# A two-dimensional Fourier filter gated by a feed-forward block: the narrow hidden tile's down products packed into row groups, the variances' roots as a power on GpSimd, and the head's steps in another order

## The chip, the cores and the metric

The kernel runs on one core of a Trainium2 chip. The metric is the device time of one execution in microseconds (us); the time before is the median of three runs. A second source is one profiled execution, in which every instruction of every engine has a start, a duration and the event that released it. The engines are PE (TensorE: matmuls, with PEld for its weight loads), DVE (VectorE), ACT (ScalarE), POOL (GpSimd) and SP (SyncE, which issues most of the DMAs). Each engine works through its own queue in the order in which it was written.

## The reference

The input `x` has 2048 rows of 512 values, all float32. Each row is normalised; the normalised rows go through two branches whose product is added to `x`.

```python
xn = (x - mean(x)) / sqrt(var(x) + 1e-5)            # per row
s  = irfft2(rfft2(xn) * (w_r + 1j * w_i))           # 2048 x 512 spectral filter
gate, up = xn @ W_gate, xn @ W_up                   # 512 -> 1376
g  = silu((gate * (gate > 0) * up) @ W_down)        # 1376 -> 512
out = x + s * g
```

## The kernel before

**Number format.** Every float32 operand of a large matmul is split into a float16 high part and a float16 low part, and a product is made of three passes: high x high, high x low and low x high (`PASSES`, line 24). A matmul here is one 128-column weight load and a stream of up to 512 columns.

**Feed-forward branch.** The 2048 rows form four blocks of 512 (`NBL`), each of four row tiles of 128. The 1376 hidden columns form eleven tiles: ten of 128 and a last one of 96 (`TAIL`, `fwidth`, line 58). For a block `c` and a tile `f`, `product` (line 683) makes gate and up in PSUM, twelve matmuls of 512 columns each; `rectify` (line 735) takes the positive part of the gate on ACT; `hidden` (line 741) multiplies on DVE and splits the result into a high part (ACT) and a low part (DVE), in the tile `h16`. `down` (line 758) then accumulates, for each row tile `i`, three matmuls of 512 columns per hidden tile into one PSUM tile `dn`; for the narrow tile these contract 96 of the 128 rows. After the eleventh tile `gate` (line 774) applies SiLU on ACT. `ff_steps` (line 782) lists these steps for blocks 1 to 3; block 0 is written out at lines 1079 to 1096.

**Spectral branch.** `fold` and `split` (lines 435 and 464) prepare pairs of row tiles on DVE and ACT, `first_stage` (line 472) makes the first transform, `fft_chunk` (line 805) eight chunks of the middle ones through DRAM, `last_stage` and `finish` (lines 965 and 1022) the inverse and the output.

**Head.** For the first two pairs of row tiles (`c` = 0 and 1) `stats` (line 318) takes mean and variance on DVE. `deviation` (line 329) forms 16 / sqrt(var + eps): a square root on ACT, and on DVE a reciprocal, one refining step and the product of mean and scale with its sign turned. `normalise` (line 370) then makes `xf`, here on ACT (`NORM`, line 37). `turn_row` (line 416) transposes each row on PE into the tile `head` and splits it into `xT`, high on ACT, low on DVE. The gate and up weights come in seven groups (tiles `raw`); `squares`, `group_scale` and `group_split` (lines 507 to 565) find a power of two for each tile and split it (tiles `m`, `sum`, `p`, `wgu`). For pairs 2 to 7 `deviations` (line 352) does four rows' roots at once on DVE, by an integer estimate and three refining steps. While PE has nothing to do in the head, `keep_busy` (line 406) gives it matmuls whose result (`idle`) nobody reads.

**Down weights.** `load_down` (line 586) loads W_down, `down_scale` (line 593) finds its scale and `down_weights` (line 615) splits each hidden tile's weights into the two halves of `wds`, high on ACT and low on DVE.

**Order.** All of this is entered as steps in a planner (`Plan`, line 77). A step has an engine, an assumed cost, names that it reads and writes, and a due time, set by hand (the constants of lines 33 to 47) or from the steps that need it. The planner goes through time, lets each engine begin the step that is due first among those that can begin, counts the buffers of each kind (`k4`: 12, `F`: 2, `gu`: 2, `dn`: 2 and so on; `F`, `gu` and `dn` lie in PSUM, an `F` tile takes two banks, the others one) and so writes one fixed order per engine. `ORDER` (line 42, empty) can replace single due times. A step with `port=True` is not planned at the same time on DVE and POOL.

Of the kernel before, what the change touches and what calls it, by code (L numbers as in the profile page):

```python
# [7 lines left out]
F16 = mybir.dt.float16  # L8
# [235 lines left out]
def kernel(ctx: ExitStack, tc: tile.TileContext, x, w_in, wd, wd_tail, wl, ew, sp, c_r, c_d, c_m, c_x, c_s, out):  # L244
# [42 lines left out]
    T = Plan({"k4": 12, "k2": 10, "h16": NFT, "xg": NBL + 1, "F": 2, "gu": 2, "dn": 2, "q": 4, "q4": 2, "mv": 4, "m": 4, "p": 4, "am": 1, "mid": 3})  # L287
# [41 lines left out]
    def deviation(c):  # L329

        tile_of(f"q{c}", "q", [P, 4, 2], F32)

        def first():
            q = T[f"q{c}"]
            DVE.tensor_scalar(q[:, 0], T[f"mv{c}"][:, :, 1], EPS, -4.0 / XS ** 2, op0=ALU.add, op1=ALU.mult)

        def last():
            ve, sq, y, t = (T[f"q{c}"][:, i, :] for i in range(4))
            DVE.reciprocal(y, sq)
            for i in range(2):  # L340
                DVE.scalar_tensor_tensor(t[:, i:i + 1], y[:, i:i + 1], ve[:, i:i + 1], y[:, i:i + 1],
                                         op0=ALU.mult, op1=ALU.mult)
            DVE.scalar_tensor_tensor(y, t, 3.0, y, op0=ALU.add, op1=ALU.mult)
            if "ACT" in NORM[c]:
                DVE.scalar_tensor_tensor(ve, T[f"mv{c}"][:, :, 0], -1.0, y, op0=ALU.mult, op1=ALU.mult)
        step("DVE", .13, first, reads=[(f"mv{c}", 0), (f"mv{c}", 1)], writes=[(f"q{c}", 0)], port=True)
        step("ACT", .11, lambda: ACT.activation(T[f"q{c}"][:, 1], T[f"mv{c}"][:, :, 1], AF.Sqrt, bias=eps, scale=4.0 / XS ** 2),
             reads=[(f"mv{c}", 0), (f"mv{c}", 1)], writes=[(f"q{c}", 1)])
        step("DVE", .78 + .14 * ("ACT" in NORM[c]), last, reads=[(f"q{c}", 0), (f"q{c}", 1)], writes=[(f"q{c}", 2)], port=True)
        return f"q{c}", 0  # L350

    def deviations(cs):


        name = f"q{cs[0]}"
        tile_of(name, "q4", [P, 3, 4], F32)

        def run():
            w, y, t = (T[name][:, i, :] for i in range(3))
            b = T[name].bitcast(I32)  # L360
            for j, c in enumerate(cs):
                DVE.tensor_scalar(w[:, 2 * j:2 * j + 2], T[f"mv{c}"][:, :, 1], EPS, 64.0 / XS ** 2, op0=ALU.add, op1=ALU.mult)
            DVE.tensor_scalar(b[:, 1, :], b[:, 0, :], -0.5, float(0x5F3759DF), op0=ALU.mult, op1=ALU.add)
            for n in range(3):
                DVE.scalar_tensor_tensor(t, y, -(4.0 ** -n), y, op0=ALU.mult, op1=ALU.mult)
                DVE.tensor_mul(t, t, w)
                DVE.scalar_tensor_tensor(y, t, 3.0, y, op0=ALU.add, op1=ALU.mult)
        step("DVE", 2.4, run, reads=[(f"mv{c}", i) for c in cs for i in range(2)], writes=[(name, 2)], port=True)
# [413 lines left out]
    def ff_steps(c, lag=6):  # L782
# [8 lines left out]
        for f, i in [(f, i) for i in range(2) for f in range(NFT - lag, e - i)] + [(e, 0), (e - 1, 1), (e, 1)]:  # L791
            down(c, f, (i,))
            if f == e:
                gate(c, i)
# [4 lines left out]
        for f, i, part in order:  # L799
            down(c, f, (i,), part)  # L800
            if f == e:
                gate(c, i, part)
# [430 lines left out]
```

## Time and profile before

| | us |
|---|---|
| median of three runs (409.93 to 410.04) | 410.02 |
| profiled execution, its own time | 409.73 |
| profiled execution, span from first to last instruction | 407.9 |
| PE busy (3056 matmuls) | 402.5 |
| DVE busy | 303.9 |
| ACT busy | 191.0 |
| POOL busy | 54.1 |

The profiled execution's own time is 1.8 us above its span, and 0.3 us below the median. PE's busy time contains 10.9 us of the `idle` matmuls, all in the first 20 us. The records of matmuls overlap (a matmul of 512 columns is shown with 379 ns, and the next starts about 216 ns later), so PE's speed is read from the distance between starts. All instructions carry the same source line, that of the helper which keeps them in order, so they are told apart by their tiles: `dn<-wds,h` is a down product, `xf<-x,q` a normalisation, `gu<-xT,wgu` a gate or up product.

### The profile page before, as it was taken

Reading aid. Unit: us, or ns where it says so; the run is one execution under the profiler, and the core shown is the slowest. Engines: PE = TensorE matmul, PEld = TensorE weight load, DVE = VectorE, ACT = ScalarE, POOL = GpSimd, SP = SyncE. Lnnn points to the kernel's source line nnn. Section 1 sums busy time; section 2 is a strip of 40 time slices with the busy share of each in tenths; the row PEclk is TensorE's granted clock in tenths of the full one; section 3 lists DMA queues with packets and bytes.
Section 4 is the critical chain, followed back from the end, with each engine's and each line's share of the span. In section 5 each row is a group of like instructions: output and inputs, shape, how many; then the busy total and the mean of one; then the engine's idle time right before and its main releaser. Section 6 shows DMA issues by size and latency. Waiting matters only on the chain.

```text
span 407.9 us, 7730 instructions
## 1 busy us (share of the span) xinstructions
PE 402.5 (99%) x3056; PEld 213.9 (52%) x3056; DVE 303.9 (74%) x648; ACT 191.0 (47%) x361; POOL 54.1 (13%) x68
## 2 busy tenths in 40 slices
PE   8999999999999999999999999999999999999996
PEld 7784444444444444446555456555554444444445
DVE  5897999999999972416985578965882329988953
ACT  5989944634435584123344434443424236442211
POOL 0000000000000000003430031500230009351400
PEclk9999999999999999999999999999999999999999
DMA  8963042007544799800005550066002598335321
GB/s 303 416 238 103 2 114 94 0 2 154 156 104 120 251 202 251 310 2 3 1 2 167 169 169 2 1 191 176 24 0 53 125 230 240 129 130 182 123 85 53
DMA packets 35237, 51.74 MB, mean 127 GB/s; under 512 B 15424, under 2 KB 17184, under 8 KB 35200
## 3 DMA queue, kind: packets, MB, share of 16 engines
q1 hardware_dynamic: 34912, 50.71, 41.6%
q8 instruction: 24, 0.39, 0.4%
q10 hardware_dynamic: 288, 0.52, 0.4%
q14 instruction: 13, 0.11, 0.1%
HBM read 35.48 MB, written 12.60 MB: 118 GB/s over the span
## 4 chain that ended last, share of the span: by engine, by line
PE 94%; ACT 2%; DVE 2%; DMA 1%; issue 0%
PE gu L70 54%; PE dn L70 27%; PE s L70 3%; PE z L70 3%; PE xx L70 3%; PE y L70 2%; PE v L70 2%; DMA x<-in_x 1%; ACT wgu L70 1%; ACT xf L70 1%; PE dn_3bb L70 0%; PE dn_3b L70 0%; DVE wgu L70 0%; DVE q L70 0%; ACT xT L70 0%; DVE st L70 0%
## 5 line engine op out<-in xcount | busy, mean ns | idle before, releaser
L70 PE MATMUL gu<-xT,wgu 128*128 128x512 f16 (+1 forms) x1032 | 214.3, 364 | 0.3 <-DVE xT L70 0.3
L70 PEld LDWEIGHTS <-wgu 128*128 128x128 f16 x1032 | 99.5, 98 | 104.3 <-issue 3.8
L70 PE MATMUL dn<-wds,h 128*128 128x512 f16 (+2 forms) x528 | 116.3, 373 | 0.0
L70 PEld LDWEIGHTS <-h 128*128 128x128 f16 (+1 forms) x594 | 54.0, 98 | 57.0 <-issue 2.6
L70 ACT ACTIVATE h<-h 128x512 f16<-128x512 f32 (+1 forms) x44 | 27.5, 628 | 66.7 <-DVE h L70 66.7
L70 POOL TENSOR_TENSOR po<-tt,tt 128x256 f32<-128x256 f32 x16 | 15.4, 964 | 273.7 <-DVE tt L70 273.7
L70 DVE TENSOR_TENSOR h<-gu,r 128x512 f32<-128x512 f32 (+2 forms) x52 | 33.6, 647 | 23.1 <-PE gu L70 20.8
L70 ACT ACTIVATE r<-gu 128x512 f32<-128x512 f32 (+1 forms) x44 | 26.1, 594 | 30.6 <-PE gu L70 30.0
L70 DVE TENSOR_TENSOR h<-h,h 128x512 f16<-128x512 f32 (+1 forms) x44 | 29.8, 689 | 7.8 <-ACT h L70 7.8
L70 POOL TENSOR_TENSOR ae<-zz 128x128 f32<-128x128 f32 (+1 forms) x32 | 26.3, 855 | 54.5 <-ACT zz L70 54.5
L70 DVE SCALAR_TENSOR_TENSOR tt<-xsp,cw,wt 128x512 f32<-128x512 f32 x32 | 25.9, 856 | 0.0
L70 ACT ACTIVATE g<-dn,cdi 128x512 f32<-128x512 f32 (+1 forms) x16 | 10.6, 673 | 26.7 <-PE dn L70 26.6
L70 DVE TENSOR_TENSOR a<-y,a 128x1024 f16<-128x1024 f32 x8 | 9.8, 1220 | 16.1 <-ACT a L70 15.9
L70 DVE TENSOR_TENSOR t<-v,t 128x1024 f16<-128x1024 f32 x8 | 9.8, 1220 | 13.2 <-ACT t L70 13.2
L70 DVE TENSOR_TENSOR sv<-sv,g 128x512 f32<-128x512 f32 (+2 forms) x18 | 11.8, 680 | 8.8 <-ACT g L70 8.8
L70 PE MATMUL gu<-xT,wgt 128*64 128x256 f16 (+1 forms) x144 | 17.0, 309 | 0.0
L70 DVE SCALAR_TENSOR_TENSOR wgu<-raw,p,wgu 128x512 f16<-128x512 f32 x20 | 14.4, 746 | 0.2 <-ACT wgu L70 0.2
L70 ACT ACTIVATE zz<-s,cwi 128x1024 f32<-128x1024 f32 x8 | 8.7, 1112 | 11.8 <-PE s L70 9.2
L70 ACT ACTIVATE wgu<-raw 128x512 f16<-128x512 f32 x20 | 12.3, 619 | 2.9 <-DMA raw<-in_w 2.9
L70 PEld LDWEIGHTS <-wgt 128*64 128x64 f16 (+1 forms) x144 | 9.6, 106 | 7.3 <-issue 1.9
L70 DVE BATCH_NORM_STATS2 st<-x 128x6 f32<-128x512 f32 x16 | 10.8, 674 | 3.4 <-DMA x<-in_x 3.4
L70 DVE TENSOR_TENSOR z<-z,z 128x1024 f16<-128x1024 f32 x8 | 9.8, 1219 | 4.7 <-ACT z L70 4.7
(138 smaller groups left out, 433.0 us busy)
## 6 DMA issues: line engine op xcount, KB each, us to landing
A_d<-t SPq DMA_DIRECT2D x16, 256.0 KB, 3.4
rw<-in_wl SPq DMA_DIRECT2D x8, 512.0 KB, 3.7
wt<-in_wl SPq DMA_DIRECT2D x8, 512.0 KB, 5.0
at<-A_d SPq DMA_DIRECT2D x8, 512.0 KB, 5.1
C_d<-t SPq DMA_DIRECT2D x16, 256.0 KB, 3.3
ct<-C_d SPq DMA_DIRECT2D x16, 256.0 KB, 7.6
xt<-in_x SPq DMA_DIRECT2D x16, 256.0 KB, 2.9
out<-xt SPq DMA_DIRECT2D x15, 256.0 KB, 2.1
```

The lines of the kernel that those rows point to most:

```text
L70: return lambda *args, **kw: self.tc.keep_in_program_order(f(*args, **kw))
```

## The change

Three things change together. The first is the narrow tile in blocks 0 to 2 (`WHOLE = 3`). Its three passes contract 3 x 96 = 288 rows, which are now laid out as 128 + 128 + 32. The first two parts are matmuls over all 128 rows; their weights stand in `wds[:, TAIL, 0]` and `wds[:, NFT, 0]`, and `hidden` places copies of the high part and the low part beside each other in `h16`. The last 32 rows (low part of hidden columns 64 to 95) of the four row tiles are stacked in a new tile `hc`, and `down_rest` multiplies them in four matmuls, one in each group of 32 rows of the array, into four PSUM banks. For that, rows 2 and 3 of blocks 0 to 2 share an `F` tile (before, block 0 only), and all four gates of a block come after `down_rest`. W_down's last 96 rows are passed in three arrangements, the tail's DMAs are now two (256 KB, and 512 KB into a `k4` tile), and `down_weights` gets two more steps on ACT and two on DVE.

The second is the root. `deviation` and `deviations` become additions of eps, a power of -0.5 and a multiplication by 16 on POOL; the first square root's table on ACT is no longer asked for, and the table of SiLU is asked for at the start.

The third is the order: pair 0 is normalised on DVE, 86 due times, most of them of the head, are replaced by `ORDER`, and several due times set by hand are different, among them those of the first stage (from 18.18 + 17.03 k to 52.05 + 13.03 k), of the folds (`FOLD_LEAD` from 92.09 to 33.39) and of the last stage (from 275.37 + 10.87 k to 311.66 + 6.53 k).

```diff
-T0, DOWN, FIRST, FIRST_STEP, MID, MID_STEP, LAST, LAST_STEP = 0.15, 43.88, 18.18, 17.03, 171.03, 5.03, 275.37, 10.87
+T0, DOWN, FIRST, FIRST_STEP, MID, MID_STEP, LAST, LAST_STEP = 0.15, 44.8, 52.05, 13.03, 170.04, 4.98, 311.66, 6.53
-FOLDS, FOLD_LEAD, MARGIN = ['DVE', 'DVE', 'DVE', 'DVE', 'DVE', 'DVE', 'DVE', 'DVE'], 92.09, 1.89
+FOLDS, FOLD_LEAD, MARGIN = ['DVE', 'DVE', 'DVE', 'DVE', 'DVE', 'DVE', 'DVE', 'DVE'], 33.39, 1.9
-NORM, TURN1 = (('ACT', 'ACT'), ('ACT', 'ACT')), 'PE'
+NORM, TURN1 = (('DVE', 'DVE'), ('ACT', 'ACT')), 'PE'
-ORDER = {}
+ORDER = {"ACT ('x0', 1)": 8.03, "DVE ('mv0', 0)": 22.85, ... "DVE ('xf0', 0)": -2.56, "DVE ('xf0', 1)": -1.23, ... "DVE ('xf0', 2)": 61.96, ...}
+SMALL = .6, .3
+WHOLE = 3
...
-    eps = cpool.tile([P, 1], F32, name="eps")
-    DVE.memset(eps, 4.0 * EPS / XS ** 2)
-    ACT.activation(warm, ones[:, 0:1], AF.Sqrt)
+    half = cpool.tile([P, 4], F32, name="half")
+    DVE.memset(half, -0.5)
+    ACT.activation(warm, ones[:, 0:1], AF.Silu)
...
-        step("DVE", .13, first, ...)
-        step("ACT", .11, lambda: ACT.activation(T[f"q{c}"][:, 1], T[f"mv{c}"][:, :, 1], AF.Sqrt, bias=eps, scale=4.0 / XS ** 2),
-        step("DVE", .78 + .14 * ("ACT" in NORM[c]), last, ...)
+        def root():
+            POOL.tensor_scalar(r(), T[f"mv{c}"][:, :, 1], EPS, None, op0=ALU.add)
+            POOL.tensor_tensor(r(), r(), half[:, 0:2], op=ALU.pow)
+            POOL.tensor_scalar(y(), r(), XS, None, op0=ALU.mult)
+        step("POOL", SMALL[0] + SMALL[1], root, ...)
+        if "ACT" in NORM[c]:
+            step("DVE", .16, lambda: DVE.scalar_tensor_tensor(shift(), T[f"mv{c}"][:, :, 0], -1.0, y(), op0=ALU.mult, op1=ALU.mult),
...
             for j, c in enumerate(cs):
-                DVE.tensor_scalar(w[:, 2 * j:2 * j + 2], T[f"mv{c}"][:, :, 1], EPS, 64.0 / XS ** 2, op0=ALU.add, op1=ALU.mult)
-            DVE.tensor_scalar(b[:, 1, :], b[:, 0, :], -0.5, float(0x5F3759DF), op0=ALU.mult, op1=ALU.add)
-            for n in range(3):
-                DVE.scalar_tensor_tensor(t, y, -(4.0 ** -n), y, op0=ALU.mult, op1=ALU.mult)
-                DVE.tensor_mul(t, t, w)
-                DVE.scalar_tensor_tensor(y, t, 3.0, y, op0=ALU.add, op1=ALU.mult)
+                POOL.tensor_scalar(r[:, 2 * j:2 * j + 2], T[f"mv{c}"][:, :, 1], EPS, None, op0=ALU.add)
+            POOL.tensor_tensor(r, r, half, op=ALU.pow)
+            POOL.tensor_scalar(y, r, XS, None, op0=ALU.mult)
...
-        step("SP", .6, lambda: SP.dma_start(wdr[:fwidth(n), NFT, :], wd_tail), writes=[("wd", NFT)], lead=22, kb=192)
+        step("SP", .6, lambda: SP.dma_start(wdr[:, NFT, :], wd_tail[:, 0, :]), writes=[("wd", NFT)], lead=22, kb=256)
+        tile_of("wrest", "k4", [P, 2, D], F32)
+        step("SP", .6, lambda: SP.dma_start(T["wrest"], wd_tail[:, 1:3, :]), writes=["wrest"], lead=22, kb=512)
...
+        first, second = wds[:, TAIL, 0, :], wds[:, NFT, 0, :]
+        step("DVE", stt(512), lambda: less(first, wdr[:, NFT, :], slice(96, P)), ...)
+        step("ACT", act(512) + .1, lambda: ACT.activation(second, T["wrest"][:, 0, :], AF.Copy, scale=sc[:, TAIL:NFT]), ...)
+        step("DVE", stt(512), lambda: less(second, T["wrest"][:, 0, :], slice(0, 64)), ...)
+        step("ACT", act(512) + .1, lambda: ACT.activation(wds[:, NFT, 1, :], T["wrest"][:, 1, :], AF.Copy, scale=sc[:, TAIL:NFT]), ...)
...
+        if f == TAIL and c < WHOLE:
+            tile_of(f"hc{c}", "hc", [P, P], F16)
+            for k, (slot, to, of) in enumerate(((0, 96, 0), (1, 0, 32), (1, 32, 64))):
+                step("ACT", act(512), lambda slot=slot, to=to, of=of: ACT.activation(h16()[to:to + 32, slot], h32()[of:of + 32], AF.Copy), ...)
+            step("DVE", dve(512), lambda: DVE.tensor_sub(h16()[64:, 1], h32()[0:64], h16()[0:64, 0]), ...)
+            def low():
+                for i in range(4):
+                    DVE.tensor_sub(T[f"hc{c}"][32 * i:32 * i + 32], h32()[64:96, i], h16()[64:96, 0, i])
+            step("DVE", .8, low, ...)
+            return
...
+                if packed:
+                    for h in range(2):
+                        matmul(t, T[f"h16_{c}_{f}"][:, h, i, :], wds[:, TAIL + h, 0, cols], start=False, stop=False)
+                    continue
...
+    def down_rest(c):
+        names = [down_name(c, i) for i in range(4)]
+        def run():
+            for i, name in enumerate(names):
+                rows = slice(32 * i, 32 * i + 32)
+                matmul(T[name][:, i - 2, :] if i >= 2 else T[name], T[f"hc{c}"][rows, :], wds[rows, NFT, 1, :], start=False, stop=True)
+        step("PE", .25, run, mode=4, reads=[f"hc{c}", "wdr"], writes=list(dict.fromkeys(names)), due=tick(.25))
...
+        if c < WHOLE:
+            down_rest(c)
+            for i in range(4):
+                gate(c, i)
```

More of the change, by code (lines that the diff above doesn't have):

```diff
@@ L383, in normalise @@
             e = engines[i]
-            step(e, .62 if e == "ACT" else pool1(512) if e == "POOL" else dve2(512), lambda i=i: run(i), reads=[*x_names(c, i), (f"mv{c}", i), (q, 2)],
+            step(e, .72 if e == "ACT" else pool1(512) if e == "POOL" else dve2(512), lambda i=i: run(i), reads=[*x_names(c, i), (f"mv{c}", i), (q, 2), (q, 0)],
                  writes=[(f"xf{c}", i)], port=e != "ACT", due=HEAD[2 * c] if c < 2 else None)
@@ L617, in down_weights @@
             e = fwidth(f)
-            step("ACT", act(512) + .1, lambda f=f, e=e: ACT.activation(wds[:e, f, 0, :], wdr[:e, f + 1, :], AF.Copy, scale=sc[:e, f:f + 1]),
+            step("ACT", act(512) + .1, lambda f=f: ACT.activation(wds[:, f, 0, :], wdr[:, f + 1, :], AF.Copy, scale=sc[:, f:f + 1]),
                  reads=[("wd", f + 1), "scd"], writes=[("wd", f)])
@@ L622, in down_weights, with less @@
                 reads=[("wd", f + 1), ("wd", f), "scd"], writes=[("wdl", f)])
+        def less(to, of, rows):
+            DVE.scalar_tensor_tensor(to[rows], of[rows], sc[rows, TAIL:NFT], to[rows], op0=ALU.mult, op1=ALU.subtract)
+        first, second = wds[:, TAIL, 0, :], wds[:, NFT, 0, :]
+        step("DVE", stt(512), lambda: less(first, wdr[:, NFT, :], slice(96, P)), port=True, reads=[("wd", NFT), ("wdl", TAIL), "scd"], writes=[("wd", TAIL)])
+        step("ACT", act(512) + .1, lambda: ACT.activation(second, T["wrest"][:, 0, :], AF.Copy, scale=sc[:, TAIL:NFT]),
+             reads=["wrest", "scd"], writes=[("wd", NFT)])
+        step("DVE", stt(512), lambda: less(second, T["wrest"][:, 0, :], slice(0, 64)), port=True, reads=["wrest", ("wd", NFT), "scd"], writes=[("wdl", NFT)])
+        step("ACT", act(512) + .1, lambda: ACT.activation(wds[:, NFT, 1, :], T["wrest"][:, 1, :], AF.Copy, scale=sc[:, TAIL:NFT]),
+             reads=["wrest", ("wd", NFT), "scd"], writes=["wdr"])
     def filter_scale(due):
@@ L770, in run @@
                            start=f == 0 and n == 0, stop=f == NFT - 1 and n == 2)
-        cost = pe(3 * len(rows), cols.stop - cols.start)
-        step("PE", cost, run, reads=[("wd", f), ("wdl", f), (f"h16_{c}_{f}", 0), (f"h16_{c}_{f}", 1)], writes=names, due=tick(cost))
+        cost = pe((2 if packed else 3) * len(rows), cols.stop - cols.start)
+        w = [("wd", f), ("wdl", f)] + [("wd", NFT), ("wdl", NFT)] * packed
+        step("PE", cost, run, reads=[*w, *((f"h16_{c}_{f}", k) for k in range(5 if packed else 2))], writes=names, due=tick(cost))
+    def down_rest(c):
[5 more added lines that the diff above has]
+        step("PE", .25, run, mode=4, reads=[f"hc{c}", "wdr"], writes=list(dict.fromkeys(names)), due=tick(.25))
     def gate(c, i, part=0):
-        name, cols = "dn0_23" if c == 0 and i >= 2 else f"dn{c}_{i}" + "b" * part, columns(c, i)[part]
+        name, cols = down_name(c, i, part), columns(c, i)[part]
         if f"g{c}" not in T.tiles:
@@ L778, in gate @@
         step("ACT", act(cols.stop - cols.start) + .1, lambda: ACT.activation(
-            T[f"g{c}"][:, i, cols], T[name][:, i - 2, :] if name == "dn0_23" else T[name], AF.Silu, scale=cdi),
+            T[f"g{c}"][:, i, cols], T[name][:, i - 2, :] if name.endswith("_23") else T[name], AF.Silu, scale=cdi),
             reads=[name, "scd"], writes=[(f"g{c}", i, part)], due=clock[0] + 4)
@@ L792, in ff_steps @@
             down(c, f, (i,))
-            if f == e:
+            if f == e and c >= WHOLE:
                 gate(c, i)
@@ L1094 @@
             down(0, f, rows)
-        for i in rows:
-            gate(0, i)
+    down_rest(0)
+    for i in range(4):
+        gate(0, i)
     for c in range(1, NBL):
@@ L1218 @@
     wd = np.asarray(B_W_down)
[L1219 removed]
+    ins = [("x", xp), ("w", np.concatenate(wp, axis=1)), ("wd", wd[:n].reshape(TAIL, P, D).transpose(1, 0, 2)), ("wdt", np.stack([wd[n + r] for r in (np.r_[0:96, 0:32], np.r_[32:96, 0:64], np.tile(np.r_[64:96], 4))], axis=1)),
            ("wl", wl), ("ew", ew), ("sp", sp), ("c_r", c_r), ("c_d", c_d), ("c_m", c_m), ("c_x", c_x), ("c_s", c_s)]
```

43 lines of the change are left out of this document (19 added, 24 removed).

## The prediction

> **What bounds the kernel now.** I read the page first: the engines' busy time, share of the span and instructions.
>
> ```profile
> PE 402.5 (99%) x3056; PEld 213.9 (52%) x3056; DVE 303.9 (74%) x648; ACT 191.0 (47%) x361; POOL 54.1 (13%) x68
> ```
>
> PE sets the time: work that leaves PE's queue after the head shortens the run one for one, if PE doesn't begin to wait. Next come the stages, each with its length, then PE, PEld, DVE, ACT and POOL busy, the clock and the DMA share.
>
> ```profile
> 10.00:15.00 5.00, 4.71 (x45) 4.03 (x43) 4.41 (x13) 5.00 (x16) 0.00 (x0) 1.00 1.02 415
> 15.00:20.00 5.00, 4.50 (x40) 3.66 (x39) 4.32 (x14) 4.75 (x11) 0.00 (x0) 1.00 1.02 414
> 30.00:50.00 20.00, 20.00 (x101) 9.81 (x100) 17.51 (x40) 18.99 (x46) 0.00 (x0) 1.00 0.16 53
> 50.00:100.00 50.00, 50.00 (x331) 23.61 (x329) 48.16 (x119) 25.11 (x39) 0.00 (x0) 1.00 0.27 68
> 100.00:200.00 100.00, 100.00 (x725) 49.38 (x724) 70.30 (x183) 44.03 (x77) 4.31 (x5) 1.00 0.52 146
> ```
>
> From 20 us PE has no gap, at full clock. Before that ACT is the full engine (5.00 and 4.75 us of 5), DVE close to it, and the DMA engines are saturated. In 50 to 100 us DVE is 96% busy, so PE runs there without waiting only because the order suits it. The head, in the chain in order of time (start, length) and in the timeline:
>
> ```profile
> 6.16 0.30 ACT q L70
> 7.46 1.52 ACT xf L70 x2
> 8.98 1.84 ACT wgu L70 x5
> 10.82 0.97 ACT xT L70 x2
> 19.87 8.02 PE gu L70 x72
> ```
>
> ```profile
> 5.94 0.18 DVE L70 BATCH_NORM_AGGREGATE mv<-st 128x2 f32<-128x6 f32 x1
> 8.47 0.37 DVE L70 TENSOR_SCALAR p<-p 128x2 int32<-128x2 int32 x2
> 9.04 0.66 PE L70 MATMUL head<-cS,xf 128*128 128x128 f32 x4
> 10.12 0.71 ACT L70 ACTIVATE wgu<-raw,p 128x512 f16<-128x512 f32 x1
> 11.83 1.03 PE L70 MATMUL gu<-xT,wgu 128*128 128x256 f16 x8
> 13.15 1.47 PE L70 MATMUL gu<-xT,wgu 128*128 128x256 f16 x12 [0.29 <-DVE xT L70]
> 14.60 1.91 PE L70 MATMUL gu<-xT,wgu 128*128 128x256 f16 x16
> 17.12 1.47 PE L70 MATMUL gu<-xT,wgu 128*128 128x256 f16 x12
> ```
>
> Pair 0's variance is ready at 6.12 us, its scale at 7.46; ACT then holds the chain alone: normalise, squares and split of weights, copies of xT. Useful products begin at 11.83 and have no gap from 19.87. In those 8.04 us PE does 8 + 12 + 16 + 12 = 48 products of 256 columns; 72 of them take 8.02 us further on, so 48 are 5.35. Two groups of transposes take about 0.5 us each (from here: issued up to the next work, 0.1 below the 0.66 shown) and the scale sums 0.1. So about 1.5 us are lost after the start, and the start is late.
>
> **Part 1, the packed tile.** What PE pays, from chain rows of undisturbed and of mode-changing work:
>
> ```profile
> 117.05 1.29 PE dn L70 x6
> 312.16 2.59 PE gu L70 x12
> 212.44 2.70 PE gu L70 x12
> 221.66 0.77 PE v L70 x12
> ```
>
> A down product costs 1.29 / 6 = 0.215 us. A narrow tile costs a block 12 of them; now 8, and one round of four in four row groups. The trace has no such row groups, but `v` runs 64 x 64 tiles: 12 products of 512 columns in 0.77 us, that is three rounds of four at 0.215 (0.645) and 0.125 for entering the mode. Products behind a change of mode cost 2.70 instead of 2.59, so leaving costs 0.11. `down_rest` then costs 0.215 + 0.125 + 0.11 = 0.45 and a block saves 4 x 0.215 - 0.45 = 0.41 us; three blocks 1.23. Bounds: if the changes of mode fall beside others', 3 x 0.645 = 1.94 saved; if the four run one after another, 0.235 lost a block, 0.7 in all.
>
> The Trainium skill, "TensorE: Matmul & The Clock Gate", section "Measured speedup vs the span model", gives 3.07 instead of 4 for four row tiles of 32 at 512 columns. By that figure the round would be an estimated 0.28 us and three blocks would save about 1.0 us; the `v` row speaks for 4, and no run here shows 32-row groups yet.
>
> What the packing adds elsewhere, by groups (busy, mean ns):
>
> ```profile
> L70 ACT ACTIVATE h<-h 96x512 f16<-96x512 f32 x4 | 2.5, 630 | 12.9 <-DVE h L70 12.9
> L70 DVE TENSOR_TENSOR xs<-ee 128x128 f32<-128x128 f32 x16 | 3.6, 283 | 0.0
> L70 DVE SCALAR_TENSOR_TENSOR wds<-wds,scd 96x512 f16<-96x512 f32 x1 | 0.7, 742 | 0.0
> L70 ACT ACTIVATE g<-dn,cdi 128x512 f32<-128x512 f32 x15 | 10.1, 686 | 23.9 <-PE dn L70 23.9
> wds<-in_wdt SPq DMA_DIRECT2D x1, 192.0 KB, 12.1
> ```
>
> Each block: three more copies on ACT (3 x 0.63 = 1.9 us), four small subtractions on DVE (4 x 0.283 = 1.1). Once: two weight steps on DVE (1.5) and two on ACT. The tail's data come last of eleven tiles, and PE has the other ten tiles' down products of four rows (40 x 0.645 = 26 us) in front, so I cost this at nothing; without that cover it is the 1.9 once a block. The four gates in one row (4 x 0.69 = 2.7 us of ACT) hold `dn` and `F`, which block c+1 needs only after six hidden tiles (6 x 2 x 2.59 = 31 us). The DMAs grow from 192 to 768 KB: 576 KB at 415 GB/s are 1.4 us, in a stretch where all DMA is saturated. They wait for no one until the down scale, but weight groups issued behind them on SP may come up to 1.4 us later; PE has the first three tiles' products (6 x 2.59 = 15.5 us) in front of those, so nothing, and at most 1.4.
>
> **Part 2, the roots.** The longest and the shortest POOL rows, a normalisation on each engine, and the first and last of the eleven refining instructions for pairs 2 and 3:
>
> ```profile
> 0.24 0.10 POOL L1222 MEMSET const-float32-0.0<- 128x1 f32 x1 [0.24 <-issue]
> 259.88 1.58 POOL L70 TENSOR_TENSOR po<-tt,tt 128x256 f32<-128x256 f32 x1 [2.75 <-DVE tt L70]
> L70 DVE TENSOR_SCALAR xf<-x,mv,q x12: 536/540/544, 71.9 to 128.8; 128x512 f32<-128x512 f32 x12
> L70 ACT ACTIVATE xf<-x,q x4: 800/808/816, 7.5 to 17.1; 128x512 f32<-128x512 f32 x4
> 67.95 0.23 DVE L70 TENSOR_SCALAR q<-mv 128x2 f32<-128x2 f32 x2
> 69.99 0.16 DVE L70 SCALAR_TENSOR_TENSOR q<-q 128x4 f32<-128x4 f32 x1
> ```
>
> The old root takes 7.46 - 6.12 = 1.34 us. The new one is three dependent POOL instructions on two values; a power is nowhere in the trace. Low 3 x 0.10 = 0.3, high 3 x 1.58 = 4.7. I take 0.45 each, 1.35 in all, nearer to the memset, because two values are nearer to its one than to 256: no change, bounds -1.0 and +3.4. Pairs 2 to 7 lose 2.2 us of DVE per two pairs (67.95 to 70.15), 6.6 in all, most of it where DVE is 96% busy; PE does not wait there, so this pays only by carrying part 1's additions. The second load of ACT's tables goes too; it stands under block 0's down products, so nothing.
>
> **Part 3, the head.** Normalising two rows on DVE ends at about 7.47 + 2 x 0.54 = 8.55 instead of 8.98, and ACT's 1.52 us, with its share of two roots, are free. Squares and weight split (1.84 us) can stand beside the normalisation, where before they stood behind it. Transposes end at about 8.55 + 0.06 + 0.66 = 9.3 and xT's second copy at 9.8: a gain of 2.0. If weight scale (ready at 8.84), split (0.71) and two copies (0.97) stay in one row on ACT, it is 10.5: a gain of 1.3. I take 1.6. Bounds from the root: up to 2.6, down to -1.8. Of the 1.5 us of gaps I take half, 0.75, since ACT's load falls and the first folds on DVE get due later; bounds 0 and 1.5. What those folds are:
>
> ```profile
> 16.78 0.68 DVE L70 TENSOR_TENSOR eo<-xf 128x510 f32<-128x510 f32 x1
> 26.47 1.29 DVE L70 TENSOR_TENSOR xs<-ee 128x128 f32<-128x128 f32 x6
> ```
>
> They are spread from 16.8 to 27.7 us, some 6 us of DVE, and go into stretches with 2.5 and 1.8 us free up to 100 us; the 100 behind have 30. Two `F` tiles carry the middle transforms, and blocks 1 and 2 now hold one of them for the rows 2 and 3 (22 x 0.645 = 14 us each); PE has other work to run, so nothing, and the price is below.
>
> **Sum.** 1.23 + 1.6 + 0.75 = 3.6 us. The profiled execution took 409.73 (span 407.9 and 1.8 around it), so 406.1; the median is 0.3 higher, so 406.4.
>
> **Rivals.**
>
> (a) The root is slow, and DVE's queue waits for it. Both normalisations of pair 0 now stand in DVE's own order behind POOL's result; behind them stand the statistics of pair 1, the scales `p` and the weight splits, which PE's first products need. At 4.7 us the first root costs 3.4 and eats the gain to 409.8. Pair 1's root adds as much again where DVE waits for it before rows 2 and 3: 1.7 to 3.4 more, 411.5 to 413. It decides from a root of about 5 us, or two of 3.2. For it: no power in the trace, and DVE and POOL disturb each other when both read:
>
> ```profile
> 343.09 0.63 DVE L70 TENSOR_TENSOR ye<-ae,zz 128x256 f32<-128x256 f32 x1
> 346.33 0.41 DVE L70 TENSOR_TENSOR ye<-zz,ae 128x254 f32<-128x254 f32 x1
> 335.85 10.28 POOL L70 TENSOR_TENSOR ae<-zz 128x128 f32<-128x128 f32 x16 [34.07 <-ACT zz L70]
> ```
>
> The sum of 256 took 0.63 us during POOL's work and 0.41 behind it. Against it: only two values. The Trainium skill, "SBUF — State Buffer", section "Who interferes with whom", has a POOL instruction and a DVE one with two SBUF inputs shut each other out completely, whoever comes second waiting; the row shows a wait of 0.22, and a POOL root of three instructions among weight splits of 0.74 would by that rule wait up to 2.2 longer.
>
> (b) The head gains nothing: weights and DMA hold the products where they are. DMA is saturated from 10 to 20 us, and DVE is at 4.3 of 5. Then 410.0 - 1.2 = 408.8.
>
> (c) The row groups run one after another: 410.0 - 2.35 + 0.7 = 408.4. The `v` row is against it.
>
> (d) The held `F` tile delays the transforms. Half the rate for 2 x 14 us is up to 14 us of delay; the last output work of DVE had this slack before the last block's gate:
>
> ```profile
> 398.74 0.69 DVE L70 TENSOR_TENSOR sv<-sv,g 128x512 f32<-128x512 f32 x1 [5.71 <-ACT g L70]
> ```
>
> A delay beyond 5.7 us shows at the end. If a third of the 14 remains, nothing; if two thirds, 9.3 - 5.7 = 3.6 and the gain is gone: 410.0. The later due time of the last stage fits some delay.
>
> **How the numbers follow.** The forecast (405 to 407.8) has 0.50, (a) 0.14 on the slower side, (b) 0.20, (c) 0.05, (d) 0.11 for no change. A measurement of this kernel tells about 0.2%, 0.8 us, from nothing, so faster is below 409.2: 0.50 + 0.20 + 0.05 = 0.75; the same 0.11; slower 0.14. At best parts 1 and 3 give 1.94 + 2.6 + 1.5 = 6.0, 404.0. I set 404.4 to 410.8, which takes in (b), (c) and (d), and leaves out (a)'s slower half.
>
> **What would show it.** The first `gu` should start at 9.8 to 10.6, and the gapless stretch at 17 to 18. POOL should show `q` between 6 and 8 us with starts 0.3 to 0.6 apart; over 1.5 is (a), with `xf` on DVE waiting for POOL. The number of down products stays, but of those over 96 rows only block 3's are left, and twelve over 32 rows appear, in three pieces of 0.3 to 0.45 in the chain; 0.9 or more is (c). PE should stay at its full length in every stage behind 20 us; a wait of PE for DVE `h` or `wds`, or of a transform for an `F` tile, would make the sum wrong by its length. If DVE's wait for the last `g` shrinks from 5.7 to nothing, (d) has happened.

## The result and the profile after

The changed kernel takes 407.99 us (median; 407.28 to 408.21), the one before 409.98 in the same comparison: a ratio of 0.9949 with a 95% interval of 0.9937 to 0.9961, a gain of 2.0 us. Forecast were 3.6 us and 406.4. The profiled execution of the changed kernel took 407.87, which is 1.86 less than the one of before; its span is 406.1.

The page's line of the engines, and the stages (each with its start and end, its length, PE, PEld, DVE, ACT and POOL busy, the clock, the DMA share and GB/s), after the change:

```profile
PE 401.1 (99%) x3056; PEld 213.9 (53%) x3056; DVE 302.4 (74%) x617; ACT 193.6 (48%) x367; POOL 57.1 (14%) x86
```

```profile
15.00:20.00 5.00, 5.00 (x49) 4.55 (x47) 4.82 (x10) 4.98 (x15) 0.00 (x0) 1.00 1.02 416
50.00:100.00 50.00, 50.00 (x292) 23.55 (x291) 46.34 (x100) 23.62 (x37) 3.12 (x4) 1.00 0.28 55
```

PE still has its full length behind 20 us; DVE in 50 to 100 us went from 48.16 to 46.34; the refining work that stood there before (67.95 to 70.15) is on POOL now. ACT is as full as before in 15 to 20 us, although it no longer normalises pair 0: a first hint that the head gained little. The plainest count of what the head delivers is the number of gate and up products that PE starts from 9 to 30 us (length, PE busy by them, their number in brackets, clock, DMA share, GB/s). Before:

```profile
9.00:30.00 21.00, 16.00 (x140) 1.00 0.87 342
```

After:

```profile
9.00:30.00 21.00, 16.25 (x139) 1.00 0.90 346
```

By 30 us PE is one product behind. The forecast's 2.35 us for the head, at 0.11 us a product, would have put it some twenty ahead. So the whole gain lies behind the head. Summing the distances between starts of successive products, from the first gate product of 512 columns (30.48 us before, 30.56 after) to the start of the last product, gives 373.60 us before and 371.72 after. Of these 1.88 us the down products, the packed ones among them, give 1.43; the `s` products, which run in 64 x 64 tiles, give 0.25, since they stand alone in eight groups (a ninth follows other products in small tiles) and no longer in eleven; 0.2 is in gate and up products, some of which pay for leaving a mode.

The packed round itself, in the table of the tile `dn` and in PE's timeline of block 0:

```profile
L72 PE MATMUL dn<-wds,hc x12: 384/384/385, 101.5 to 310.2; 32*128 32x512 f16 x12
```

```profile
101.46 0.40 PE L72 MATMUL dn<-wds,hc 32*128 32x512 f16 x4
101.79 1.04 PE L72 MATMUL gu<-xT,wgu 128*128 128x512 f16 x4
```

Twelve products over 32 rows, four in each round; from the first of a round to the next work are 101.79 - 101.46 = 0.33 us, entering included, and the same 0.33 in the other two rounds. Four in a row would be 0.86. The twelve gate and up products behind this round stand in the chain with

```profile
101.86 2.70 PE gu L72 x12
```

where undisturbed ones took 2.59, so leaving costs 0.11 here too.

POOL's first root and what stands around it in the head:

```profile
6.09 0.23 POOL L72 TENSOR_SCALAR q<-mv 128x2 f32<-128x2 f32 x1 [5.67 <-DVE mv L72]
6.40 0.73 POOL L72 TENSOR_TENSOR q<-q,half 128x2 f32<-128x2 f32 x1
6.85 0.63 ACT L72 ACTIVATE wgu<-raw 128x512 f16<-128x512 f32 x1 [1.16 <-DMA raw<-in_w]
7.21 0.25 POOL L72 TENSOR_SCALAR q<-q 128x2 f32<-128x2 f32 x1
7.87 0.97 DVE L72 TENSOR_SCALAR xf<-x,mv,q 128x512 f32<-128x512 f32 x2
9.22 1.04 PE L72 MATMUL head<-cS,xf 128*128 128x128 f32 x8
9.88 0.38 DVE L72 TENSOR_SCALAR p<-p 128x2 int32<-128x2 int32 x2
10.30 1.09 ACT L72 ACTIVATE xT<-head 128x512 f16<-128x512 f32 x2 [1.25 <-PE head L72]
12.05 1.31 PE L72 MATMUL gu<-xT,wgu 128*128 128x256 f16 x8 [0.26 <-ACT wgu L72]
```

The root ends at 7.46, at the same time as before. The normalised rows are ready at 8.84, but the transposes start at 9.22 to 9.38 and end at 10.27, with ACT waiting 1.25 us for them, and the first gate product starts at 12.05 instead of 11.83. The chain in order of time (start, length, what) says why PE was late:

```profile
1.04 7.12 PE idle L72 x44
8.15 0.12 PE sum L72 x2
8.27 1.11 PE idle L72 x10
9.38 0.89 PE head L72 x8
16.44 0.87 PE idle L72 x8
17.31 2.66 PE gu L72 x24
```

The chain of before ran through ACT here. Now it runs through 44 `idle` products, which exist only to keep PE busy: the first scale sum stands in PE's queue behind them, and the transposes behind ten more. How fast they went is seen in windows of one microsecond of PE (length, busy, products, clock, DMA share, GB/s). Before:

```profile
3.00:4.00 1.00, 1.00 (x8) 1.00 1.01 369
4.00:5.00 1.00, 1.00 (x12) 1.00 1.05 404
```

After:

```profile
3.00:4.00 1.00, 1.00 (x6) 1.00 0.97 348
4.00:5.00 1.00, 1.00 (x6) 1.00 1.01 381
5.00:6.00 1.00, 1.00 (x9) 1.00 1.01 356
6.00:7.00 1.00, 1.00 (x11) 1.00 1.04 375
```

In both kernels the products come at half rate first, 213 ns from start to start, and then at full rate, 109 ns. In this execution the change to full rate came about 1.7 us later. The column of the granted clock shows 1.00 throughout, so only the count and the distances show it. Last, what ACT waited for in the first 20 us (us in all, times, longest), before and after:

```profile
ACT wgu L70 <- DMA raw<-in_w: 2.9, 1, 2.9
```

```profile
ACT wgu L72 <- DMA raw<-in_w: 4.7, 3, 2.8
ACT xT L72 <- PE head L72: 1.2, 1, 1.2
```

The 1.52 us that ACT was freed of turned into 1.8 us more of waiting for raw weights, and 1.2 for PE.

### The profile page after: what moved, and what is told of

Same layout as the page of the kernel before. It is cut to its first block, busy times and chain, and to the rows that moved or that the text cites. A ratio compares the mean times of both kernels' runs of the same rounds, so it can differ in the third digit from the quotient of the medians.

```text
span 406.1 us, 7727 instructions
## 1 busy us (share of the span) xinstructions
PE 401.1 (99%) x3056; PEld 213.9 (53%) x3056; DVE 302.4 (74%) x617; ACT 193.6 (48%) x367; POOL 57.1 (14%) x86
## 4 chain that ended last, share of the span: by engine, by line
PE 98%; DVE 0%; ACT 0%; issue 0%
PE gu L72 55%; PE dn L72 27%; PE s L72 3%; PE z L72 3%; PE xx L72 3%; PE idle L72 2%; PE y L72 2%; PE v L72 2%; PE dn_3bb L72 0%; PE dn_3b L72 0%; PE head L72 0%; ACT xT L72 0%; PE sum L72 0%; DVE xT L72 0%; ACT g L72 0%
## 5 line engine op out<-in xcount | busy, mean ns | idle before, releaser
L72 PE MATMUL dn<-wds,h 128*128 128x512 f16 (+3 forms) x516 | 113.4, 372 | 0.0
L72 PEld LDWEIGHTS <-h 128*128 128x128 f16 (+1 forms) x582 | 52.8, 98 | 55.8 <-issue 2.6
L72 ACT ACTIVATE h<-h 128x512 f16<-128x512 f32 (+2 forms) x53 | 32.9, 629 | 58.2 <-DVE h L72 58.0
L72 DVE TENSOR_TENSOR h<-h,h 128x512 f16<-128x512 f32 (+2 forms) x44 | 30.0, 698 | 8.5 <-ACT h L72 8.4
L72 POOL TENSOR_TENSOR ae<-zz 128x128 f32<-128x128 f32 (+1 forms) x32 | 21.1, 694 | 63.0 <-ACT zz L72 58.1
L72 POOL TENSOR_SCALAR q<-mv 128x2 f32<-128x2 f32 x8 | 3.0, 370 | 120.1 <-DVE mv L72 120.1
L72 ACT ACTIVATE a<-y 128x1024 f16<-128x1024 f32 x8 | 8.2, 1024 | 15.7 <-PE y L72 15.7
L72 ACT ACTIVATE z<-z 128x1024 f16<-128x1024 f32 x8 | 8.2, 1024 | 12.6 <-PE z L72 12.6
```

Source lines behind the costliest of these rows:

```text
L72: return lambda *args, **kw: self.tc.keep_in_program_order(f(*args, **kw))
```

## The experiments

Four things were to be told apart: what the packing gives, whether POOL's root is a cost or a gain, whether weights and DMA hold the head, and what the order written into `ORDER` does. Each kernel was timed beside the kernel before, whose medians in the three comparisons are 409.89, 409.85 and 409.79, so a difference between kernels of different comparisons is uncertain by some 0.1 to 0.2 us. "Head" is the start of the first gate product of 512 columns, "rest" the time from there to the start of the last product; both are worked out from the starts of PE's products in the profiled execution, whose own time stands in brackets.

| kernel | median | ratio to before, 95% | head | rest | (its own time) |
|---|---|---|---|---|---|
| before | 409.98 | 1 | 30.48 | 373.60 | (409.73) |
| after | 407.99 | 0.9937 to 0.9961 | 30.56 | 371.72 | (407.87) |
| after, once more | 408.01 | 0.9938 to 0.9963 | 30.71 | 371.71 | (408.01) |
| packing alone | 409.15 | 0.9975 to 0.9993 | 30.77 | 373.05 | (409.40) |
| after without packing | 409.47 | 0.9986 to 1.0003 | 30.75 | 373.37 | (409.99) |
| the same, packed weights still loaded | 413.48 | 1.0072 to 1.0099 | 30.17 | 373.38 | (413.32) |
| roots alone | 412.29 | 1.0037 to 1.0062 | 30.03 | 375.28 | (410.97) |
| after, `ORDER` empty | 407.00 | 0.9920 to 0.9945 | 29.57 | 371.57 | (406.72) |
| `ORDER` empty, slower roots | 408.01 | 0.9944 to 0.9972 | 30.76 | 371.57 | (408.01) |
| `ORDER` empty, old roots | 409.00 | 0.9970 to 0.9992 | 31.80 | 372.11 | (409.50) |
| after, folds' due times left out | 413.13 | 1.0069 to 1.0096 | 32.65 | 374.50 | (412.83) |
| after, fewer idle products | 407.06 | 0.9921 to 0.9946 | 30.02 | 371.72 | (407.31) |
| `ORDER` empty, fewer idle products | 406.59 | 0.9905 to 0.9932 | 29.57 | 371.57 | (406.79) |
| before, fewer idle products | 409.75 | 0.9989 to 1.0007 | 30.48 | 373.60 | (409.73) |

### The packing

The packed tail in the kernel before, with before's roots, normalisation, due times of the stages and empty `ORDER`, and `FOLD_LEAD` and `MARGIN` of after:

```diff
 # after, but:
-ORDER = {"ACT ('x0', 1)": 8.03, ...}
+ORDER = {}
-NORM, TURN1 = (('DVE', 'DVE'), ('ACT', 'ACT')), 'PE'
+NORM, TURN1 = (('ACT', 'ACT'), ('ACT', 'ACT')), 'PE'
 # T0 ... LAST_STEP, deviation, deviations and normalise as before
```

> The kernel before plus the packed narrow tile, with the later folds of the change (lead 33.39 instead of 92.09), but with the roots, the normalisation on ACT and all other due times of before. Theory (the change's gain is all PE work behind the head: the first 512-column product starts at 30.5 us before and after, and from there PE needs 1.9 us less, 1.4 of it in the down products): 1.3 to 1.5 us faster than before, 408.6, with the first 512-column product at 30.5 +- 0.3. Rival (the packing itself pays 1.2 and the rest comes from the head or the roots): 408.8 with an unchanged number of mode changes. Rival (folds in the head cost PE): first 512-column product at 29.5 or earlier, 407.6.

Measured: 409.15 (409.05 to 409.82), 0.7 us faster than before, about half of what was expected. PE's waits, summed (us, times, longest), show two that neither other kernel has:

```profile
PE y L72 <- DVE xsp L72: 0.3, 1, 0.3
PE s L72 <- DVE t L72: 0.2, 1, 0.2
```

The second has the packing's own DVE work ahead of it in DVE's queue, the last of the four small subtractions and then `t`, in the chain in order of time:

```profile
97.74 0.28 DVE hc L72
98.03 1.30 DVE t L72 x2
```

With this order PE also changes into a tiling mode 33 times, where before and after do so 29 times (not counting the few products of a single row or column). At the prediction's 0.125 + 0.11 = 0.235 us each, four more are an estimated 0.94; with the waits' 0.5 that is 1.4, and its rest is 1.33 us longer than after's. So the packed round costs what it should (0.33 us in each of its three blocks here too), and what it saves is partly spent on where the planner puts the other work.

The opposite, after with the tail unpacked:

```diff
-WHOLE = 3
+WHOLE = 0
 # no down_rest(0); block 0's gates behind their rows
```

> The changed kernel with no block packed (rows 2 and 3 of block 0 alone share an F tile again, gates behind their rows as before); roots and order of the change stay. Theory (packing is 1.4 of the 2.0 us): 409.4, 1.4 slower than the changed kernel and 0.6 faster than before. Rival (head and roots gain, the packing's work elsewhere eats its own gain): 408.2, within 0.3 of the changed kernel.

Measured: 413.48 (ratio 1.0086, 1.0072 to 1.0099), far outside. The chain's end tells why:

```profile
402.75 1.02 PE dn_3bb L72 x18
405.23 3.74 DMA wrest<-in_wdt
408.99 0.73 ACT wds L72
409.74 0.74 DVE wds L72
```

The load of the packed weights and their scaling stood in the kernel still, though nobody used them; without a user they had no due time and came at the very end: the span is 411.4 us, and 408.0 in the run below that leaves them out. This says nothing of the packing. Without that load and its four steps:

```diff
-WHOLE = 3
+WHOLE = 0
-        tile_of("wrest", "k4", [P, 2, D], F32)
-        step("SP", .6, lambda: SP.dma_start(T["wrest"], wd_tail[:, 1:3, :]), ...)
 # and without the steps that write first, second and wds[:, NFT, 1, :]
```

> The changed kernel with no block packed, as in the run without packing, but the tail's two extra arrangements are now neither loaded nor scaled (there they stood unused behind the last output and made the end 4 us later). Theory (packing is worth 1.65 us: 373.4 instead of 371.7 from the first 512-column product to the last product): 409.5, 1.6 slower than the changed kernel. Rival (packing 1.2, as worked out before the result): 409.1. Rival (its work on ACT and DVE costs as much as it saves): 407.9.

Beside it, the changed kernel once more:

> The changed kernel itself, on one chip with the three that follow. 407.9 +- 0.3; first 512-column product at 30.3 to 30.8 us, and from there to the last product's start 371.7.

Measured: 409.47 (409.07 to 410.44) without packing, 408.01 (407.13 to 408.27) with it, both as expected. The packing is worth 1.46 us by medians and 373.37 - 371.71 = 1.66 by the rests. Without it roots and order together stand at 0.9995 of before (0.9986 to 1.0003): no gain that can be measured.

### The root

POOL's roots alone in the kernel before (with `half` and the warm-up of SiLU; nothing else of the change):

```diff
 # before, but deviation and deviations as after:
+            POOL.tensor_scalar(r(), T[f"mv{c}"][:, :, 1], EPS, None, op0=ALU.add)
+            POOL.tensor_tensor(r(), r(), half[:, 0:2], op=ALU.pow)
+            POOL.tensor_scalar(y(), r(), XS, None, op0=ALU.mult)
```

> The kernel before with the roots as powers on GpSimd and nothing else changed: same due times, pair 0 still normalised on ACT, no packing. Theory (the POOL chain of three takes 1.35 us like the old root, and the 6.6 us of DVE it frees lie under PE): 410.0 +- 0.3, first 512-column product at 30.5 +- 0.4. Rival (ACT is what bounds the head, and two square roots less on it show): 0.6 faster, 409.4. Rival (POOL's root is disturbed by DVE's two-input work): 0.5 to 2 slower.

Measured: 412.29 (410.97 to 412.37), 2.4 us slower, where no change was expected. The profiled execution is the fastest of the five and only 1.24 us slower than the one of before, so its trace accounts for half of the loss. Its head is 0.45 us earlier than before, and its rest is 1.68 longer. In the last stage of the timeline:

```profile
344.10 0.69 DVE L71 TENSOR_TENSOR xt<-xt,sv 128x512 f32<-128x512 f32 x1 [0.95 <-DMA xt<-in_x]
346.86 5.34 PE L71 MATMUL gu<-xT,wgu 128*128 128x512 f16 x24 [0.79 <-DVE h L71]
355.25 2.10 PE L71 MATMUL gu<-xT,wgu 128*128 128x512 f16 x9 [0.46 <-ACT r L71]
```

No root is within 200 us of these rows. The planner has put the output work in another order; DVE waits 0.95 us for a row of `x`, and PE 1.25 for DVE and ACT behind that. In this execution the edit at the start is paid for at the end, through an order that the due times set by hand no longer suit. The other half of the loss, in the four slower runs, no trace shows.

The price of a slow root, with `ORDER` empty, as two more powers whose results are not used ahead of each power of pairs 0 and 1:

```diff
+            for _ in range(2):
+                POOL.tensor_tensor(T[f"q{c}"][:, 3, :], r(), half[:, 0:2], op=ALU.pow)
             POOL.tensor_tensor(r(), r(), half[:, 0:2], op=ALU.pow)
```

> The changed kernel without the replaced due times, and with two further powers on GpSimd (0.73 us each by the trace, results unused) ahead of each root of pairs 0 and 1, the order of all engines kept. Theory (DVE's queue stands behind POOL's root of pair 0, and the chain behind it sets the first product): first product 1.2 to 1.5 us later than the 11.57 of the run without replaced due times, but only part of it is left at the first 512-column product (29.57 there), since weights and DMA landings stand beside it: 30.2 +- 0.4, 407.7. Rival (the root is the head's only bound): 31.0, 408.5. Rival (weight groups bound the head): 29.6, 407.0.

```profile
6.37 2.27 POOL L72 TENSOR_TENSOR q<-q,half 128x2 f32<-128x2 f32 x3
9.01 1.00 DVE L72 TENSOR_SCALAR xf<-x,mv,q 128x512 f32<-128x512 f32 x2 [1.77 <-POOL q L72]
```

Measured: 408.01, 1.0 us more than the same kernel without the extra powers. DVE's queue waits 1.77 us for POOL where it waited 0.25, the normalisation starts at 9.01 instead of 7.64, 1.4 us later, and the head ends 1.19 later. The result lies between the expected 407.7 and the rival's 408.5. In this execution the first scale sum was late too, at 8.14 against 7.26, so not all of the 1.19 need be the root's. The times tell more: all five runs took 407.98 to 408.22, and the fastest without the extra powers 406.62. So the place of rival (a)'s cost is right, and of 1.46 us more of root 1.0 (by medians) to 1.36 (by the fastest runs) is paid.

The old roots under the new due times, `ORDER` empty:

```diff
 # after, ORDER = {}, but deviation, deviations, normalise and eps as before
```

> The changed kernel without the replaced due times, with the roots of before (square root on ACT, the rest on DVE; integer estimate for pairs 2 to 7); packing, pair 0 on DVE and the other due times stay, but the planner's order shifts with the other costs. Theory (the root takes 1.34 us either way): head within 0.4 us of the run without replaced due times, 407.0 to 407.4, if the order behind it keeps PE fed. Rival (POOL's root frees ACT and DVE in the head): 0.5 to 1 slower, first 512-column product at 30.1 to 30.6. Rival (the 6.6 us of DVE work that return in the stretch where DVE is full stall PE): waits of PE behind 30 us, 1 to 3 slower.

Measured: 409.00 (408.52 to 410.24), 2.0 us slower than with POOL's roots, where at most 0.4 was expected. Its fastest run is 1.9 us slower than the fastest with them, so chance doesn't explain it. Its profiled execution has the latest change to full rate of all (first scale sum at 9.04 in the chain), a rest 0.54 longer and a wait of PE for `xT` of 0.7 us. How much of the 2.0 is the root itself, and how much the order that the planner makes around it, these runs don't separate.

### The head

After with `ORDER` empty, so that the planner's own due times hold:

```diff
-ORDER = {"ACT ('x0', 1)": 8.03, "DVE ('mv0', 0)": 22.85, ...}
+ORDER = {}
```

> The changed kernel without the 86 replaced due times; packing, roots, pair 0 on DVE and the other due times stay. Theory (the order of the head brings nothing by itself): 408.0 +- 0.4, first 512-column product at 30.5 +- 0.5. Rival (the order hides a loss of 1 to 2 us that the roots or pair 0 on DVE bring to the head): 409 to 410, first 512-column product at 31.5 to 32.5.

Measured: 407.00 (406.62 to 407.85), 1.0 us faster than the changed kernel; neither the theory nor the rival had a gain. The gate and up products from 9 to 30 us, and its chain:

```profile
9.00:30.00 21.00, 16.89 (x147) 1.00 0.85 346
```

```profile
1.04 6.38 PE idle L72 x44
7.42 0.12 PE sum L72 x2
```

Eight products more than after by 30 us, some of them already of 512 columns: 30.56 - 29.57 = 0.99 us. This execution had an early change to full rate, so the 0.99 holds both the order and the clock; the two are taken apart below.

One guess at what in `ORDER` costs it was the folds: in after, DVE folds `xf` at 15.3 to 16.7 us ahead of a weight split, while PE runs the eight idle products of 16.44. Here the 19 due times of the folds are left out and 67 kept:

```diff
-ORDER = {... "DVE ('xf0', 2)": 61.96, ...}   # the entries of xf (2), eo, ee and xs
```

> The changed kernel with the 19 replaced due times of the folds dropped (they put pieces of pair 0's fold on DVE at 15.3 to 16.7 us, ahead of a weight split for which PE runs idle products), the other 67 kept. Theory (those fold pieces cost the head about half of the 1.0 us that the order costs): first 512-column product at 30.0, 407.4. Rival (the whole loss is the late scale of the first weights, ready at 10.26 instead of 9.25): no change, 30.5 and 407.9. Rival (the folds are the whole loss): 29.6, 407.0.

Measured: 413.13 (412.62 to 413.75), 5.1 us slower than after, which none of the three cases had. PE's waits:

```profile
PE gu L72 <- ACT wgu L72: 1.1, 2, 0.9
PE gu L72 <- DVE wgu L72: 0.9, 2, 0.6
PE dn L72 <- DVE wds L72: 0.8, 1, 0.8
```

With these 19 due times gone and the other 67 kept, the planner's order makes PE wait for weights in the head and for the down weights behind it; with all 86 gone, above, PE waits for neither. The run doesn't tell what the folds cost in the changed kernel.

Then the idle products. The first nine steps of `keep_busy` issue two products each instead of three, so 35 and not 44 stand ahead of the first scale sum (in the kernel before 36 and not 45). In the changed kernel:

```diff
-... for _ in range(m)], ...
+... for _ in range(2 if m == 3 else 1)], ...
```

> The changed kernel with the same 35 instead of 44 idle products, its 86 replaced due times kept. Theory (the order's loss in the two profiles of the changed kernel is the late clock of these executions): 407.2, about as fast as its fastest runs, and within 0.3 us of the kernel without replaced due times. Rival (the order itself loses 0.5 or more): 407.3 to 407.5 while the run without it gives 406.6. Rival (idle products don't matter): 408.0.

With `ORDER` empty:

> The changed kernel without the replaced due times, and with 35 instead of 44 idle products in PE's queue ahead of the first scale sum (each of the first nine steps issues two instead of three; every other instruction and all orders stay). Theory (the first scale sum stands in PE's queue behind 44 idle products, which run at half rate until the clock opens, 3.6 to 5.9 us after the start by the profiles so far; so the sum goes at 7.3 to 8.4 and carries that chance into the head): the sum at 6.6 to 7.1 in every execution, first 512-column product at 29.0 to 29.6, 406.6, and the runs within 0.4 us of each other instead of 1.2. Rival (the spread and the start come from DMA landings): no change, 407.0 with the same spread. Rival (the clock opens later with fewer idle products): 0.5 to 1 slower.

In the kernel before:

> The kernel before with the same 35 instead of 44 idle products. Theory (there the scale of the first weights waits for the statistics on DVE until 8.28 us, 1 us behind the sum, and ACT holds the chain, so the clock's chance is hidden): 409.8 +- 0.2, and the head's gain of the change with fewer idle products is then 409.8 less the packing and stage grouping's 1.9 less the time measured. Rival (the idle products bound the head before as well): 409.0.

Measured: 407.06 in the changed kernel (0.95 faster), 406.59 with `ORDER` empty (0.41 faster), 409.75 in the kernel before (ratio 0.9998, nothing). PE in windows of a microsecond and the chain with `ORDER` empty:

```profile
5.00:6.00 1.00, 1.00 (x7) 1.00 1.05 372
6.00:7.00 1.00, 1.00 (x9) 1.00 1.05 386
```

```profile
1.04 6.59 PE idle L72 x35
7.63 0.12 PE sum L72 x2
```

Half rate lasted beyond 6 us here, longer than in the profile of after, and the sum still came at 7.63, against 8.15; it was expected at 6.6 to 7.1. The two profiles of the changed kernel show how the sum is passed on: in the second it came 0.15 us later (8.30), and so did the first product of 512 columns (30.71 against 30.56). So the late change to full rate reaches the end of the kernel through the idle products in front of the sum, in the changed kernel and not in the one before, whose chain goes through ACT.

The gain seems to be that of the executions whose full rate comes late; only the profiled ones show when it came, so for the others this is inferred from their times. With `ORDER` empty the two profiles, one with an early change and 44 idle products and one with a late change and 35, both have their head at 29.57, and the fastest runs lie close, 406.62 and 406.49; but the slowest took 407.85 with 44 and 406.79 with 35. In the changed kernel the fastest of nine runs with 44 took 407.13 and the fastest with 35 took 406.86; one of the five with 35 still took 408.05, which no trace explains. Between the two kernels with fewer idle products the order alone is left: 407.06 against 406.59, heads of 30.02 and 29.57, so `ORDER` costs some 0.45 us. Part of it shows in when the first scale `p` is ready: at 10.26 in after (its row above), where DVE takes pair 1's second statistics first, and a microsecond earlier with `ORDER` empty:

```profile
8.87 0.38 DVE L72 TENSOR_SCALAR p<-p 128x2 int32<-128x2 int32 x2
```

The version with `ORDER` empty and fewer idle products is faster than both kernels: 406.59, ratio 0.9918 (0.9905 to 0.9932).

## Why the prediction was right or wrong

The time moved as forecast and fell inside the range, but little more than half of the forecast gain is there. The range of 404.4 to 410.8 was wide enough to take in most of the rivals; the forecast's own case, 405 to 407.8, was missed by 0.2 us. The case that happened is the forecast's packing, somewhat better than its sum, with rival (b)'s head, which gains nothing; that the time lies as near to 406.4 as it does is luck in that sense.

**Part 1: right, and somewhat too low.** 1.23 us were forecast, 1.46 to 1.66 measured, inside the bounds of 0.7 lost and 1.94 saved. The step "`down_rest` then costs 0.215 + 0.125 + 0.11 = 0.45" holds: 0.33 for entering and the round, and 0.11 for leaving, give 0.44. The `v` row was the right neighbour, and rival (c) is out. The Trainium skill, "TensorE: Matmul & The Clock Gate", section "Measured speedup vs the span model", would make entering and round an estimated 0.28 + 0.125 = 0.405 by its 3.07; the 0.33 here is within 0.01 of a fourfold gain. What the sum lacked was that the order around the packed tile also decides how many groups of small tiles stand alone. From before to after that gave 0.25 us in the `s` products; about half of it, 0.12, also goes when after is left unpacked, and the rest belongs to the other due times. Packing alone has four such changes more instead.

"What the packing adds elsewhere" at nothing: right. PE waits nowhere behind 20 us in after. The cover is thin, though: with packing alone the four small subtractions on DVE, in the stretch where DVE was 96% busy before, stand ahead of a wait of PE of 0.2 us.

**Part 2: the duration right, "no change" not fully shown.** 1.35 us were forecast for the root and 7.46 - 5.99 = 1.47 measured, from the variance at 5.81 + 0.18 to the end of POOL's third instruction; the starts lie 0.31 and 0.81 apart, outside 0.3 to 0.6 only for the one behind the power. That the sum fits is in part luck: three equal shares of 0.45 were guessed, and the power takes three times as long as either of the others. Pairs 2 to 7 have longer powers:

```profile
L72 POOL TENSOR_TENSOR q<-q,half x5: 717/1027/1504, 6.4 to 129.3; 128x4 f32<-128x4 f32 x3, 128x2 f32<-128x2 f32 x2
```

DVE waits for POOL once there, 1.8 us, and PE not at all. The Trainium skill, "SBUF — State Buffer", section "Who interferes with whom", agrees with the long ones: beside a subtraction of two tiles on DVE (128.49 to 129.15) POOL's small addition, begun at 128.66, took 0.57 us, and 0.22 elsewhere. In the head the three instructions showed nothing of it, and the 2.2 us that the prediction worked out from it did not occur. That DVE's queue would stand behind the root, rival (a), is right in kind: 0.25 us with `ORDER` empty, and 1.0 to 1.36 us of time once the root is 1.46 longer. Whether the root is worth nothing or more than that stays open, since the old one under the new due times is 2.0 us slower.

**Part 3: wrong, both terms.** "I take 1.6" for the earlier start, and 0.75 for the gaps; the profiled execution has 0 by the head, and roots and order without packing give nothing measurable. Three steps of the working failed.

"Transposes end at about 8.55 + 0.06 + 0.66 = 9.3": they end at 10.27. The rows were 0.29 late, because in after a statistic of pair 1, which waits 1.04 us for its row of `x`, stands ahead of them in DVE's queue. Above all, the working took PE as free because it had only idle products to do. PE's queue is in order, so idle products in front of the sum and of the transposes are work like any other, at half rate until the clock opens. In before this was covered by ACT's chain (fewer idle products there change nothing); moving ACT's work away uncovered it. The price was not in the sum. It is 0.95 us by medians here and 0.27 by the fastest runs, since it hangs on when the full rate comes.

"If weight scale (ready at 8.84) ...": it was ready at 10.26. The late sum is not the reason, for DVE was busy with the rows until 8.84 and the sum began at 8.15; `ORDER` puts pair 1's second statistics before it. The prediction had the statistics of pair 1 behind the normalisations, and didn't place `p` against them. With `ORDER` empty it was ready at 9.25, and ACT then splits the weights before it copies `xT`, not behind. The written order costs some 0.45 us in all.

"Since ACT's load falls": ACT's freed time became waits for raw weights (2.9 us to 4.7) and for the transposes. That is rival (b)'s "weights and DMA hold the products where they are". It is half right: the DMA share is 1.02 in both kernels from 15 to 20 us, but with `ORDER` empty and fewer idle products the head is 0.91 us earlier under the same DMA. So the queue of PE and the written order held that much of it. What holds the other 1.4 of the forecast's 2.35, weights or something else, these runs don't tell.

The markers: the first gate product at 9.8 to 10.6 was the right one to look at, and 12.05 showed the miss. "The gapless stretch at 17 to 18" was a poor one. It begins at 17.31 as forecast, yet PE has done 24 narrow products by then, and with 2.56 us at 0.11 about 47 by 19.87, where before had 48. A stretch without gaps tells nothing of what was done before it.

**Rival (d): its sign appeared, not its price.** The last output work of DVE waits less for its gate, 1.28 us instead of 5.71:

```profile
396.94 0.69 DVE L72 TENSOR_TENSOR sv<-sv,g 128x512 f32<-128x512 f32 x1 [1.28 <-ACT g L72]
```

That is 4.4 us of slack, but 1.8 of them are gone because the gate itself comes earlier. DVE's work ahead of it ended at 393.03 before and at 395.66 in after, 2.6 later, less than the 4.7 of "a third of the 14". And most of that isn't the packing's: after without packing, with the same due times, shows

```profile
399.29 0.69 DVE L72 TENSOR_TENSOR sv<-sv,g 128x512 f32<-128x512 f32 x1 [4.41 <-ACT g L72]
```

so its DVE was done at 394.88, and the packing adds 0.8. With packing alone, under before's due times, it is 396.52, 3.5 later than before. In all of them the last gates still come after DVE's other work.

**The sum.** 1.46 for the packing and about 0.5 more of 2.0, against 1.23 + 1.6 + 0.75. With `ORDER` empty and fewer idle products the same packing, roots and normalisation give 409.79 - 406.59 = 3.2 us, near the 3.6 but by another sum: 373.60 - 371.57 = 2.03 behind the head, where 1.23 were forecast, and 0.91 in the head, where 2.35 were. So some 0.9 us of the head were there to be had, and the idle products and the order in which the changed kernel issues its steps gave them back.

## What to carry to other kernels

Before work is taken off the chain, follow the engine that receives it: filler in an in-order queue is free only while another chain is longer, and it must be short enough that its slow rate doesn't matter when that chain shrinks. To judge a head, count the useful products started by a fixed time, rather than the first product or the first stretch without gaps. Where a planner writes the order, an edit is tried with the due times that belong to it; one part alone under the other part's due times measured mostly the order here.

## What the runs showed of the hardware

How long PE's first products run at half rate differs from execution to execution. The last product at half rate started 3.6 us after the span's start in the profile of before and 6.8 us in the latest of the others, that with the old roots under `ORDER` empty, with the same idle products issued from 1.04 us on, while the granted clock is shown as 1.00. The Trainium skill, "TensorE: Matmul & The Clock Gate", section "What's actually happening", has the clock start at half and open after about 3.4 us of sustained work, and says that this varies by run; the traces agree with the half rate and the variation, but here it took 2.6 to 5.8 us from the first product.

A power on POOL takes 0.73 us for two values in each partition and 1.03 to 1.50 for four, the longer ones beside DVE's work on two tiles; that is three to four times an addition or a multiplication of the same size (0.23 and 0.25).

Four products over 32 rows in four row groups run as one: 0.33 us with entering the mode, where one product over a whole tile takes 0.215.
